# Four interleaved attention layers on one core: the linear layers' second pass in halves of the array's rows

## The chip, the cores and the metric

The kernel runs on one core of one Trainium2 chip. The metric is the device time of one execution in microseconds (us), the median of several runs. PE is the matrix engine, PEld its weight loads, DVE the vector engine, ACT the scalar engine, POOL the GpSimd engine and SP the engine that issues most DMAs.

## The reference

Four layers follow each other, A, B, A, B, each with a residual sum, on x of 2048 tokens and 512 features, 32 heads of 16. The A layers are linear attention; the change is in them. (B is softmax attention in four segments with a compressive memory; it is not touched.)

```
def _A_ref(x, wqkv, w_phi, wo):          # x is layer-normed
    q, k, v = split((x @ wqkv))          # each [heads 32, tokens 2048, 16]
    pq = einsum("hsd,hdf->hsf", q, w_phi);  pk = the same of k
    phi_q = concat([softmax(pq), softmax(-pq)])      # 32 features a head
    phi_k = concat([softmax(pk), softmax(-pk)])
    kv = einsum("hsf,hsd->hfd", phi_k, v);  z = sum over s of phi_k
    num = einsum("hqf,hfd->hqd", phi_q, kv)
    den = einsum("hqf,hf->hq", phi_q, z) + 1e-6
    return (num / den) @ wo
x = x + _A_ref(_layernorm(x), ...)
```

All numbers are fp32; large products are split into a high and a low fp32r part and done as three products.

## The kernel before, in words

A layer A works in tiles of 128 tokens, 16 of them (NT). Its first pass makes keys, values and the raw queries' features, and sums over all tokens, for each head, 32 features by 17 columns (16 of kv and one of z). These sums become KN, a tile of 128 rows (4 heads of 32 features) by 8 groups by 4 x 17 columns, where each head's rows are zero outside its own 17 columns.

The second pass, `pass2`, is what the change touches. For each tile i it does these steps, in this order in the text of the program:

1. `turn`: the divided outputs o of tile i-1 are transposed on PE (four 128x128 blocks into one PSUM bank), ACT copies the high part, DVE subtracts the low part (tiles oh, ol).
2. `exp` on ACT of the features of tile i+2.
3. For i of 12 and more, `transposed(i+1)` stands here; see step 5.
4. KN: two halves of 4 groups. Each group is two products, of 128 feature rows by 64 tokens each, against all 68 columns of KN's group, at column positions 0 and 64 of the array. After each half, `weigh` divides by the 17th column on DVE (reciprocal r, then a product into o).
5. For i = 0 and i = 3 to 11, `transposed(i+1)`: the features of tile i+1 (1024 columns) are transposed on PE in eight 128x128 blocks into the two banks of the PSUM tile lg, and ACT copies them out (tile P).
6. `differences` on POOL for tile i+3, then `scale_q` of tile i+2: sums es on DVE (behind its exp), the ratio rr on DVE, and a product on POOL that scales one half of the features. Only after it can `transposed` of that tile run.
7. Loads of the raw features of tile i+4 and of the residual rows.
8. `out_proj` of tile i-1: 12 products of 128x128 by 512 on PE, then a sum with the residual rows x on DVE straight from PSUM, and the store. For i = 1 and 2, `transposed(i+1)` stands behind it.

The second pass is a generator; after most of the steps it yields. The main loop takes its first 110 steps (A20), and between them, at the step numbers in STEPS, one step of the next B layer's opening (weights, layer norm, four transposes a tile). One tile is nine steps. The remaining steps are dealt out into early slots of layer B.

The order of the instructions on each engine is fixed: `held` ties every PE instruction to the one traced before it, and the wrapper `Ordered` does so for DVE, ACT, POOL and SP. So each engine works in the order in which the program text calls it. PSUM has the tags g (4 banks), lg (one tile of two banks), mx and my (one bank each). All matrix products are recorded at the line of `mm` (L177), transposes at that of `tp` (L181), and everything on the four wrapped engines at L155.

Of the kernel before, what the change touches and what calls it, by code (L numbers as in the profile page):

```python
# [7 lines left out]
F32 = mybir.dt.float32  # L8
F32R = mybir.dt.float32r
# [9 lines left out]
P = 128  # L19
NSEG = 4  # L20
NC = D // P
NT = T // P
VW = DH + 1
# [6 lines left out]
OO = 4  # L30
UU = 3
MT = 1
G = 4
# [68 lines left out]
def interleave_kernel(ctx, tc, x_in, a_wqkv, a_wphi, a_wo, b_wq, b_wk, b_wv, b_wo, b_beta,  # L102
                      c_ident, c_mask, c_bd, out):
    nc = tc.nc
    MUL, ADD, SUB, MAX, MIN = ALU.mult, ALU.add, ALU.subtract, ALU.max, ALU.min
# [10 lines left out]
    def nm(s):  # L116
        uid[0] += 1
        return f"{s}_{uid[0]}"

    def T2(tag, bufs, dt=F32, shape=(P, 512)):  # L120
        return sp.tile(list(shape), dt, tag=tag, bufs=bufs, name=nm(tag))

    def PS(tag, bufs, shape=(P, 512)):
        return ps.tile(list(shape), F32, tag=tag, bufs=bufs, name=nm(tag))
# [7 lines left out]
    def wait(f):  # L132

        if put_off[0] is None:
            f()
        else:
            put_off[0].append(f)

    def behind(i, j):

        tc.add_manual_dep(i.ins, j.ins.name,
                          mybir.DependencyInfo(mybir.DependencyClass.NoSync, mybir.DependencyReason.DATA),
                          reason="keeps order")
# [19 lines left out]
    dve, act, pool, sync = [Ordered(e) for e in (nc.vector, nc.scalar, nc.gpsimd, nc.sync)]  # L163

    def held(i):

        if last[0] is not None:
            behind(i, last[0])
        last[0] = i
        return i  # L170

    work = [0.0]

    def mm(*a, **k):
        n = a[0].free_size()
        work[0] += n / 2.26 if k["rhs"].dtype == F32R else (n * 2 / 2.4 + 25 if "tile_position" in k else 2 * max(112, n * 2 / 2.4))
        return held(nc.tensor.matmul(*a, **k))  # L177

    def tp(*a):
        work[0] += 108  # L180
        return held(nc.tensor.transpose(*a))  # L181

    def dma(out, in_):
        sync.dma_start(out=out.bitcast(F32), in_=in_.bitcast(F32))

    ident = cp.tile([P, P], F32, name="ident")
# [248 lines left out]
    def mm3(po, lhs, rhs, kcs=range(NC)):  # L435

        for kc in kcs:
            for n, (a, b) in enumerate(((0, 0), (0, 1), (1, 0))):
                mm(po, lhsT=lhs(a, kc), rhs=rhs(b, kc), start=(kc == kcs[0] and n == 0),
                   stop=(kc == kcs[-1] and n == 2))  # L440
            if kc < kcs[-1]:
                yield
# [32 lines left out]
    def turn(ot):  # L475

        o = [T2("oh", OO, F32R), T2("ol", OO, F32R)]
        pt = PS("g", G)
        for c, block in enumerate(ot):
            tp(pt[:, c * P : (c + 1) * P], block, ident)  # L480
        pt, hi, lo = [t[:, 0 : len(ot) * P] for t in (pt, *o)]
        act.copy(hi, pt)
        wait(lambda: dve.tensor_tensor(out=lo, in0=pt, in1=hi.bitcast(F32), op=SUB))
        return o

    turns = [0]

    def residual(xsrc, i, spare, every=4):
# [5 lines left out]
    def out_proj(x, xdst, i, o, w):  # L494
        po = PS("g", G)
        yield from mm3(po, lambda a, kc: o[a][:, kc * P : (kc + 1) * P], lambda b, kc: w[b][:, kc, :])

        def end():
            dve.tensor_tensor(out=x, in0=po, in1=x, op=ADD)
            sync.dma_start(out=xdst[i], in_=x)  # L500
        wait(end)
        yield

    def out_pair(tiles, xdst, w, soon, late, w0=0, w1=D):
# [15 lines left out]
    def weigh(out, p, eps, add, eng=pool):  # L520

        n, G = out.shape[1], out.shape[2]
        r = T2("r", 4, shape=(P, n, G))
        den = p[:, :, :, DH]
        if eps:
            dve.tensor_scalar(r, den, eps, None, op0=ADD)
            den = r
        dve.reciprocal(r, den)
        rb = r.unsqueeze(3).broadcast_to([P, n, G, DH])
        if not add:  # L530
            dve.tensor_tensor(out=out, in0=p[:, :, :, 0:DH], in1=rb, op=MUL)
            return
        t = T2("wt", 1, shape=(P, n, G, DH))
        dve.tensor_tensor(out=t, in0=p[:, :, :, 0:DH], in1=rb, op=MUL)
        eng.tensor_tensor(out=out, in0=out, in1=t, op=ADD)
# [71 lines left out]
    def differences(p, mm):  # L607

        pv = p.rearrange("p (h f) -> p h f", f=DH)
        e = T2("P4", NP4, shape=(P, H, 2, DH))  # L610
        pool.tensor_tensor(out=e[:, :, 0, :], in0=pv,
                                in1=mm[:, 0, :].unsqueeze(2).broadcast_to([P, H, DH]), op=SUB)
        pool.tensor_tensor(out=e[:, :, 1, :],
                                in0=mm[:, 1, :].unsqueeze(2).broadcast_to([P, H, DH]), in1=pv, op=SUB)
        return e

    def exp(e):
        ef = e.rearrange("p h s f -> p (h s f)")
        act.activation(ef, ef, AF.Exp)
# [24 lines left out]
    class LayerA:  # L644
# [267 lines left out]
        def pass2(self):  # L912

            KN = self.KN
            phT = {}

            def transposed(i):

                if i >= NT:
                    return
                ef = self.e.pop(i).rearrange("p h s f -> p (h s f)")
                phT[i] = T2("P4", NP4, shape=(P, 8, P))
                pt = PS("lg", 1, (P, 2, 512))
                for half in range(2):
                    for q in range(4):
                        g = 4 * half + q
                        tp(pt[:, half, q * P : (q + 1) * P], ef[:, g * P : (g + 1) * P], ident)
                    if half == 1:  # L930
                        act.copy(phT[i].rearrange("p g t -> p (g t)"), pt.rearrange("p h x -> p (h x)"))
                    yield

            yield from transposed(0)
            o = None
            self.rest = []
            for i in range(NT):
                if 0 < i <= NT - 4:
                    oT = turn([o[:, c * P : (c + 1) * P] for c in range(NC)])
                    yield  # L940
                soon = [i + 2] if i < NT - 5 else [i + 2, i + 3] if i == NT - 5 else [i + 3]
                soon = [n for n in soon if n < NT]
                for n in soon:
                    exp(self.e[n])
                o = T2("ot", OT) if NT - 4 <= i else T2("U", UU)
                if i >= NT - 4:
                    yield from transposed(i + 1)
                f = phT.pop(i)
                for half in range(2):
                    pn = PS("g", G)  # L950
                    pv = pn[:, 0 : 16 * VW].rearrange("p (g h e) -> p g h e", g=4, h=4)
                    for q in range(4):
                        g = 4 * half + q
                        for a in (0, 64):
                            mm(pn[a : a + 64, q * 4 * VW : (q + 1) * 4 * VW], lhsT=f[:, g, a : a + 64],
                               rhs=KN[:, g].rearrange("p h e -> p (h e)"), start=True, stop=True,
                               tile_position=(0, a))
                    weigh(o[:, half * 256 : half * 256 + 256].rearrange("p (g h d) -> p g h d", g=4, h=4),
                          pv, 0.0, False)
                    yield  # L960
                if i == 0 or 2 < i < NT - 4:
                    yield from transposed(i + 1)
                if i == 0:
                    self.begun(3)
                for n in [i + 3] if i < NT - 6 else [i + 3, i + 4] if i == NT - 6 else [i + 4]:
                    if n < NT:
                        self.e[n] = differences(*self.raw.pop(n))
                for n in soon if i != 1 else ():
                    scale_q(self.e[n])
                for n in [i + 4] if i < NT - 7 else [i + 4, i + 5] if i == NT - 7 else [i + 5]:  # L970
                    self.load_q(n)
                if i < NT - 4:
                    ahead = residual(self.xsrc, i, ("ot", OT))
                else:
                    self.rest.append(o)
                if 0 < i <= NT - 4:
                    yield from out_proj(x, self.xdst, i - 1, oT, self.wo)
                if 0 < i < 3:
                    yield from transposed(i + 1)
                if i == 1:  # L980
                    scale_q(self.e[i + 2])
                x = ahead
# [621 lines left out]
```

## Time and profile before

| | us |
|---|---|
| median of 3 runs | 1316.24 |
| lowest, highest | 1312.12, 1317.13 |
| the profiled execution, its time | 1313.56 |
| its span, first to last instruction | 1311.8 |
| busy in it: PE | 1269.2 |
| DVE | 1075.4 |
| ACT | 835.4 |
| POOL | 758.6 |

The page's groups name an instruction by its tiles, written <- read. `g<-KN,P` are the products with KN, `lg<-ident,P` the transposes of features, `g<-ident,U` those of outputs, `g<-w,oh` and `g<-w,ol` the output projection, `es` and `rr` the sums and ratios on DVE, `P<-P,rr` the scaling on POOL. A fp32 product is recorded as two. In the timeline a row gives start, length, engine, line, operation, tiles and a count of merged instructions; in square brackets stand the engine's idle time before it and what ended that.

### The profile page before, as it was taken

The page shows a single profiled execution, that of the slowest core. Times are in us where ns is not written, and L with a number is a line of the kernel's source. Part 1 is how long each engine was busy: PE and PEld are TensorE (multiplying, and loading weights), DVE is VectorE, ACT ScalarE, POOL GpSimd, SP SyncE. Part 2 cuts the span into 40 slices and gives each one's busy share as a digit, 9 for nine tenths or more (in the row PEclk, how much of TensorE's full clock was granted, in tenths as well). Part 3 has the DMA queues.
Part 4 walks back from the last instruction along what each step waited for, and adds up shares of the span by engine and source line. Part 5 has one row for each costly group of instructions (what it writes and reads, how often), then busy time and mean ns, then how long its engine had stood idle before and what let it go on. Part 6 is the DMA issues. An engine that isn't in the chain of part 4 may idle for free.

```text
span 1311.8 us, 41989 instructions
## 1 busy us (share of the span) xinstructions
PE 1269.2 (97%) x16488; PEld 991.8 (76%) x16488; DVE 1075.4 (82%) x3499; ACT 835.4 (64%) x1210; POOL 758.6 (58%) x1124
## 2 busy tenths in 40 slices
PE   7999989999999999999999999899999999999987
PEld 6887878877777777777668887787877777777765
DVE  4776778788998998998857767787899899898895
ACT  5556435648788788776644433465678878877754
POOL 2568755425757768666324446563356766766653
PEclk9999999999999999999999999999999999999999
DMA  6387538545655545545441103565546545544432
GB/s 212 105 318 257 171 126 245 168 121 156 186 160 153 160 126 141 159 134 156 131 161 65 65 33 130 169 202 153 154 127 208 173 130 153 143 137 114 122 84 81
DMA packets 134420, 196.59 MB, mean 150 GB/s; under 512 B 15440, under 2 KB 61648, under 8 KB 133456
## 3 DMA queue, kind: packets, MB, share of 16 engines
q1 hardware_dynamic: 133408, 193.80, 48.9%
q8 instruction: 131, 2.15, 0.7%
q14 instruction: 65, 0.53, 0.1%
q10 hardware_dynamic: 816, 0.11, 0.1%
HBM read 101.05 MB, written 39.85 MB: 107 GB/s over the span
## 4 chain that ended last, share of the span: by engine, by line
PE 79%; DVE 14%; ACT 2%; issue 2%; DMA 2%; POOL 1%; SPq 0%; DVEq 0%; ACTq 0%; POOLq 0%
PE g L177 62%; PE lg L177 6%; PE g L181 4%; PE mx L177 3%; DVE g L155 2%; DVE U L155 2%; PE lg L181 2%; DVE mx L155 2%; DVE my L155 1%; ACT P L155 1%; PE my L177 1%; DVE es L155 1%; POOL P L155 1%; DVE mxs L155 1%; DMA P<-in 1%
## 5 line engine op out<-in xcount | busy, mean ns | idle before, releaser
L155 ACT ACTIVATE P<-lg 128x1024 f32<-128x1024 f32 x316 | 324.3, 1026 | 97.7 <-PE lg L177 75.9
L155 POOL TENSOR_SCALAR_AFFINE_SELECT P<-P 128x256 f32<-128x256 f32 (+1 forms) x448 | 190.8, 444 | 228.7 <-ACT P L155 209.3
L155 DVE CUSTOM_DVE_ANT_0 g<-g,mask 128x128 f32<-128x128 f32 (+3 forms) x392 | 189.4, 537 | 7.2 <-PE g L177 6.7
L155 DVE CUSTOM_DVE_ANT_0 mx<-mx,mask 128x512 f32<-128x512 f32 (+2 forms) x316 | 158.6, 502 | 38.1 <-PE my L177 26.3
L177 PE MATMUL g<-hh,wqk 64*128 64x512 f32 (+1 forms) x960 | 185.0, 392 | 0.7 <-SPq L155 0.3
L177 PE MATMUL g<-w,oh 64*128 64x512 f32 (+2 forms) x848 | 163.5, 382 | 3.1 <-ACT oh L155 2.6
L155 DVE CUSTOM_DVE_ANT_0 my<-my,mask 128x512 f32<-128x512 f32 (+2 forms) x316 | 163.3, 517 | 0.0
L177 PE MATMUL lg<-e,e 64*128 64x512 f32 (+1 forms) x1010 | 147.1, 344 | 7.6 <-ACT P L155 7.5
L177 PE MATMUL g<-P,v 128*32 128x128 f32 (+3 forms) x2064 | 151.7, 433 | 0.2
L177 PE MATMUL g<-w,hh 64*128 64x512 f32 (+1 forms) x672 | 143.2, 395 | 2.5 <-ACT w L155 1.3
L155 DVE DVE_READ_ACCUMULATOR2_ANT mxs<- 128x1 f32 x1024 | 142.4, 139 | 0.0
L177 PEld LDWEIGHTS lg<-e,e 64*128 64x128 f32 x1010 | 93.4, 184 | 51.7 <-ACT P L155 20.1
L177 PEld LDWEIGHTS g<-hh,wqk 64*128 64x128 f32 (+1 forms) x960 | 102.7, 185 | 18.1 <-SPq L155 1.6
L177 PEld LDWEIGHTS g<-P,v 128*32 128x32 f32 x2064 | 65.5, 109 | 60.9 <-issue 53.3
L177 PEld LDWEIGHTS g<-w,oh 64*128 64x128 f32 (+1 forms) x848 | 96.2, 188 | 19.8 <-ACT oh L155 3.5
L177 PE MATMUL g<-hl,wqk 64*128 64x512 f32 (+1 forms) x480 | 103.8, 389 | 0.0
L177 PE MATMUL g<-w,ol 64*128 64x512 f32 (+2 forms) x424 | 102.7, 379 | 0.5 <-DVE ol L155 0.5
L155 ACT COPY tb<-g 128x512 f32<-128x512 f32 (+1 forms) x132 | 71.2, 576 | 43.9 <-PE g L177 42.1
L177 PEld LDWEIGHTS g<-w,hh 64*128 64x128 f32 (+1 forms) x672 | 82.9, 187 | 19.2 <-ACT w L155 1.6
L177 PE MATMUL g<-w,hl 64*128 64x512 f32 (+1 forms) x336 | 88.7, 392 | 0.0
L155 DVE TENSOR_REDUCE es<-P 128x64 f32<-128x1024 f32 x64 | 77.3, 1209 | 13.1 <-ACT P L155 13.1
L155 POOL TENSOR_TENSOR ta<-tb,ta 128x512 fp32r<-128x512 f32 x60 | 76.3, 1292 | 14.0 <-ACT ta L155 11.2
(163 smaller groups left out, 2944.6 us busy)
## 6 DMA issues: line engine op xcount, KB each, us to landing
e<-ta SPq DMA_DIRECT2D x384, 128.0 KB
wqk<-wqk SPq DMA_DIRECT2D x128, 256.0 KB
x<-x SPq DMA_DIRECT2D x48, 256.0 KB
pq<-tb SPq DMA_DIRECT2D x24, 256.0 KB
tb<-pq SPq DMA_DIRECT2D x24, 256.0 KB
x<-xr SPq DMA_DIRECT2D x22, 256.0 KB
xr<-x SPq DMA_DIRECT2D x20, 256.0 KB
x<-in SPq DMA_DIRECT2D x16, 256.0 KB
```

The costliest lines, as they stand in the source:

```text
L155: i = f(*a, **k)
L177: return held(nc.tensor.matmul(*a, **k))
L181: return held(nc.tensor.transpose(*a))
```

## The change

- `tp_halves` is new: a block of 128 rows is transposed as two halves of 64 rows, at row positions 0 and 64 of the array, into two different PSUM banks.
- `transposed` and the new `turn_halves` use it: 16 half transposes for the features, 8 for the outputs. The outputs' halves go to the banks mx and my instead of g, and are copied by two ACT copies and two DVE subtractions of 128x256. The B layer keeps using `turn`.
- KN: each group is two products again, but now each takes 64 feature rows (two heads) by all 128 tokens, against the 34 columns of these two heads, at row positions 0 and 64; the two go to two banks of g. The division of both stands behind the second half.
- `transposed(i+1)` stands ahead of KN for i of 3 and more (it was behind it for 3 to 11).
- `out_proj`: ACT copies the product to a tile y (tag U), POOL adds the residual rows, then the store.

```
+    def tp_halves(outs, in_):
+        work[0] += 74
+        for row, out in zip((0, 64), outs):
+            held(nc.tensor.transpose(out, in_[row : row + 64], ident[row : row + 64, row : row + 64],
+                                     tile_position=(row, 0)))
...
+    def turn_halves(o):
+        hi, lo = T2("oh", OO, F32R), T2("ol", OO, F32R)
+        pts = [PS(t, 1)[:, 0 : NC * 64] for t in ("mx", "my")]
+        for c in range(NC):
+            tp_halves([pt[:, c * 64 : (c + 1) * 64] for pt in pts], o[:, c * P : (c + 1) * P])
+        views = [[t.rearrange("p (c r x) -> p r c x", c=NC, r=2)[:, r] for t in (hi, lo)]
+                 + [pts[r].rearrange("p (c x) -> p c x", c=NC)] for r in range(2)]
+        for h, _, pt in views:
+            act.copy(h, pt)
+        def low():
+            for h, l, pt in views:
+                dve.tensor_tensor(out=l, in0=pt, in1=h.bitcast(F32), op=SUB)
+        wait(low)
+        return hi, lo
...
     def out_proj(x, xdst, i, o, w):
...
-        def end():
-            dve.tensor_tensor(out=x, in0=po, in1=x, op=ADD)
-            sync.dma_start(out=xdst[i], in_=x)
-        wait(end)
+        y = T2("U", UU)
+        act.copy(y, po)
+        pool.tensor_tensor(out=x, in0=y, in1=x, op=ADD)
+        sync.dma_start(out=xdst[i], in_=x)
         yield
...
                 for half in range(2):
-                    for q in range(4):
-                        g = 4 * half + q
-                        tp(pt[:, half, q * P : (q + 1) * P], ef[:, g * P : (g + 1) * P], ident)
+                    for g in range(4 * half, 4 * half + 4):
+                        tp_halves([pt[:, r, g * 64 : (g + 1) * 64] for r in range(2)], ef[:, g * P : (g + 1) * P])
                     if half == 1:
-                        act.copy(phT[i].rearrange("p g t -> p (g t)"), pt.rearrange("p h x -> p (h x)"))
+                        act.copy(phT[i].rearrange("p g (r t) -> p r g t", r=2),
+                                 pt.rearrange("p r (g t) -> p r g t", g=8))
...
-                    oT = turn([o[:, c * P : (c + 1) * P] for c in range(NC)])
+                    oT = turn_halves(o)
...
-                if i >= NT - 4:
+                if 2 < i:
                     yield from transposed(i + 1)
                 f = phT.pop(i)
+                pns = [PS("g", G)[:, 0 : 16 * VW] for _ in range(2)]
                 for half in range(2):
-                    pn = PS("g", G)
-                    pv = pn[:, 0 : 16 * VW].rearrange("p (g h e) -> p g h e", g=4, h=4)
-                    for q in range(4):
-                        g = 4 * half + q
-                        for a in (0, 64):
-                            mm(pn[a : a + 64, q * 4 * VW : (q + 1) * 4 * VW], lhsT=f[:, g, a : a + 64],
-                               rhs=KN[:, g].rearrange("p h e -> p (h e)"), start=True, stop=True,
-                               tile_position=(0, a))
-                    weigh(o[:, half * 256 : half * 256 + 256].rearrange("p (g h d) -> p g h d", g=4, h=4),
-                          pv, 0.0, False)
+                    for g in range(4 * half, 4 * half + 4):
+                        for r, pn in enumerate(pns):
+                            row = slice(64 * r, 64 * r + 64)
+                            mm(pn[:, g * 2 * VW : (g + 1) * 2 * VW], lhsT=f[row, g, :],
+                               rhs=KN[row, g, 2 * r : 2 * r + 2, :].rearrange("p h e -> p (h e)"),
+                               start=True, stop=True, tile_position=(64 * r, 0))
+                    if half == 1:
+                        for r, pn in enumerate(pns):
+                            weigh(o.rearrange("p (g r h d) -> p r g h d", g=8, r=2, h=2)[:, r],
+                                  pn.rearrange("p (g h e) -> p g h e", g=8, h=2), 0.0, False)
                     yield
-                if i == 0 or 2 < i < NT - 4:
+                if i == 0:
                     yield from transposed(i + 1)
```

## The prediction, made before the changed kernel was run

> **What bounds the kernel now.** I read the page's shares first, then the windows of the second pass tile by tile, then one tile in the timeline.
>
> ```profile
> span 1311.8 us, 41989 instructions
> PE 1269.2 (97%) x16488; PEld 991.8 (76%) x16488; DVE 1075.4 (82%) x3499; ACT 835.4 (64%) x1210; POOL 758.6 (58%) x1124
> ```
>
> ```profile
> core 0: us, PE busy (x) PEld busy (x) DVE busy (x) ACT busy (x) POOL busy (x), PEclk, DMA share, GB/s
> 204.24:209.60 5.36, 5.36 (x60) 4.53 (x57) 4.23 (x10) 2.56 (x4) 1.98 (x2) 1.00 0.87 241
> ...
> 198.88:248.73 49.85, 49.45 (x492) 41.34 (x489) 42.86 (x94) 27.81 (x37) 29.49 (x36) 1.00 0.64 199
> 178.94:250.85 71.91, 67.75 (x717) 56.99 (x717) 60.05 (x129) 37.60 (x49) 43.20 (x50) 0.98 0.55 169
> 820.88:890.46 69.58, 66.53 (x717) 55.66 (x717) 58.09 (x125) 37.94 (x49) 42.87 (x50) 1.00 0.55 175
> ```
>
> PE is busy 97% of the span. The second pass of the two linear layers runs alone (with the next layer's opening) from 178.94 to 250.85 and from 820.88 to 890.46. From the feature turns of tile 4 at 198.88 to those of tile 13 at 248.73 there are nine tiles in 49.85 us, with PE idle for 0.4; a plain tile takes 5.36 us. Counting PE alone would be natural, but one tile shows a second chain close behind.
>
> ```profile
> 207.69 1.06 POOL L155 TENSOR_TENSOR P<-P,rr 128x512 f32<-128x512 f32 x1 [2.53 <-DVE rr L155]
> 207.97 0.60 PE L181 MATMUL g<-ident,U 128*128 128x128 f32 x4
> 208.50 1.17 PE L177 MATMUL g<-KN,P 128*64 128x68 f32 x32
> 209.60 1.09 PE L181 MATMUL lg<-ident,P 128*128 128x128 f32 x8
> 210.44 0.71 PE L177 MATMUL g<-w,oh 128*128 128x512 f32 x2
> 209.83 0.25 DVE L155 RECIPROCAL r<-g 128x16 f32<-128x16 f32 x1
> 211.08 1.21 DVE L155 TENSOR_REDUCE es<-P 128x64 f32<-128x1024 f32 x1
> 212.71 0.19 DVE L155 TENSOR_TENSOR rr<-rr,es 128x32 f32<-128x32 f32 x1
> 213.04 1.06 POOL L155 TENSOR_TENSOR P<-P,rr 128x512 f32<-128x512 f32 x1 [1.27 <-DVE rr L155]
> 213.33 0.60 PE L181 MATMUL g<-ident,U 128*128 128x128 f32 x4
> 214.96 1.09 PE L181 MATMUL lg<-ident,P 128*128 128x128 f32 x8
> ...
> 226.09 0.86 PEld L181 LDWEIGHTS lg<-ident,P 128*128 128x128 f32 x8 [0.48 <-POOL P L155]
> ```
>
> This is i = 5: outputs of tile 4 turned (207.97), tile 5 times KN (208.50), features of tile 6 turned (209.60), output projection until 213.33. On DVE, tile 5's outputs are divided from 209.83, and only behind that come tile 7's sums (es, 211.08), its ratio rr, and Pool's scaling, 213.04 to 214.10. Tile 7's features are turned at 214.96, 0.86 after. At 226.09 the turn already waits 0.48 for Pool. From the end of KN's products (208.50 + 1.17 = 209.67) to the end of the scaling: 4.43 us. Before the change this is no loop of one tile: the turn stands behind KN, so a late turn(i+1) does not delay KN(i), the head of the next scaling.
>
> **The change part by part.**
>
> *The turn of tile i+1 moves ahead of KN(i), for i = 3 to 11 (it stood there already from i = 12).* Now turn(i+1) needs the scaling issued in iteration i-1; KN(i) stands behind turn(i+1) on PE, as does the output projection; the division of tile i waits for KN(i); on DVE es(i+2) stands behind the division; and turn(i+2) waits for its scaling. The loop closes once a tile: turn, KN, then the 4.43 us above. The generators' steps per tile stay nine, so the next layer's opening falls at the same steps; none falls between KN's second half and es.
>
> *KN by half rows.* Prices:
>
> ```profile
> L177 PEld LDWEIGHTS lg<-e,e 64*128 64x128 f32 x1010 | 93.4, 184 | 51.7 <-ACT P L155 20.1 <-issue 13.0 <-ACT ta L155 4.1
> L177 PEld LDWEIGHTS g<-e,w 128*128 128x128 f32 x192 | 35.7, 188 | 8.2
> L177 PEld LDWEIGHTS g<-KN,P 128*64 128x64 f32 x1024 | 33.4, 138 | 12.5 <-ACT P L155 8.6 <-issue 2.7 <-DVE ot L155 0.3
> L177 PEld LDWEIGHTS g<-mem,tb 128*32 128x32 f32 x3072 | 31.5, 109 | 12.5 <-DVE mxs L155 9.2 <-issue 3.3
> L181 PEld LDWEIGHTS lg<-ident,P 128*128 128x128 f32 x256 | 28.1, 141 | 7.2 <-POOL P L155 4.4 <-issue 0.9
> L177 PE MATMUL g<-mem,tb 128*32 128x34 f32 x3072 | 36.9, 199 | 2.8 <-DVE mxs L155 2.8
> L177 PE MATMUL lg<-phibd,e 128*128 128x128 f32 x32 | 4.1, 280 | 0.0
> ```
>
> Before, 16 products per tile (two passes each, 32 records) load 64 columns and stream 68. After, again 16 products and 32 records, but each loads 128 columns of 64 rows and streams 34. Loads go by columns: 109 ns for 32, 138 for 64, 188 for 128; and half the rows save next to nothing (184). So the stream shrinks and the load grows by 184 - 138 = 46 to 50 ns. KN now takes 208.50 to 209.60, 1.10 us for 16 pairs, 69 ns a pair. If the pair is paced by its load, 16 x 48 = 0.77 is added: 1.94 us to the last product's end in place of 1.17. Lower end: the loads hide wholly and only 34-column streams count, 36.9 / 3072 = 12 ns, 32 of them 0.38 plus some 0.2 of drain, 0.58. Upper end: phibd's full 128-column products, 4.1 / 32 = 128 ns a pair, 2.05. I take 1.94, as the 64x128 load is the row nearest to it.
>
> The Trainium skill ("TensorE: Matmul & The Clock Gate", section "LDWEIGHTS (loading the stationary operand)") says the same against this change: a load takes its columns over 1.2 ns, whatever the rows. By it a pair grows by 53 ns where I took 48 and KN to 2.02, the total about 1343; the rows 184 and 188 agree.
>
> *Turns by halves.* A turning load of 128 columns (141) lasts no longer than KN's of 64 (138), and the stream halves to 64 columns; so I take KN's pair of today, 69 ns, against 0.84 for eight (209.60 to the next product at 210.44): features 8 x 0.069 = 0.55, outputs 0.28 for about 0.43. Bounds: no gain, 0.84; or 34-column pace, 0.2. PE gains 0.45 a tile here and loses 0.77 in KN.
>
> *Copies and residual sums.*
>
> ```profile
> L155 DVE TENSOR_TENSOR ol<-g,oh 128x512 fp32r<-128x512 f32 x32 | 21.8, 687 | 7.6 <-ACT oh L155 7.5
> L155 DVE TENSOR_TENSOR U<-g,r 128x256 f32<-128x256 f32 x48 | 20.4, 424 | 1.6
> L155 DVE TENSOR_TENSOR xr<-g,xr 128x512 f32<-128x512 f32 x12 | 8.3, 689 | 7.7 <-PE g L177 7.7
> L155 ACT COPY U<-g 128x512 f32<-128x512 f32 x32 | 19.0, 593 | 35.7 <-PE g L177 32.5 <-issue 3.2
> L155 POOL TENSOR_TENSOR xr<-tb,xr 128x512 f32<-128x512 f32 (+1 forms) x18 | 22.7, 1262 | 0.0
> ```
>
> The low parts in two halves cost DVE 2 x 0.424 for 0.687, 0.16 more, spent while DVE waits for KN: nothing. The halved ACT copies add at most one start (bounded by 0.59), under KN too: nothing, since the exponentials then end before the division does. The 24 residual sums leave DVE (0.69 each), at a place where DVE waits anyway: no gain. ACT gets 24 copies of 0.59 and Pool 24 sums of 1.26. On Pool the sum stands behind the scaling of the same iteration and ahead of the next two differences (each as wide as the scaling's 1.06): 1.26 + 2.12 after a scaling is over well within a loop of 6.9, before the next ratio comes. SP's store waits for Pool's sum instead of DVE's; the loads queued behind it feed later tiles. All hidden by the longer loop; without that cover the Pool sum would be the 1.26. The products' output in two banks per tile, divided only after both halves, starts the first division at KN's end; the 4.43 is counted from there.
>
> *The sum.* Loop = 0.55 + 1.94 + 4.43 = 6.92 us, against 49.85 / 9 = 5.54 now; PE's own work, 5.36 - 0.45 + 0.77 = 5.68, fits inside, so PE idles about 1.2 a plain tile. The first loop's start hangs on KN(2):
>
> ```profile
> 178.94 1.17 PE L177 MATMUL g<-KN,P 128*64 128x68 f32 x32 [1.50 <-DVE KN L155]
> 182.14 1.57 PE L181 MATMUL lg<-ident,P 128*128 128x128 f32 x8 [2.03 <-POOL P L155]
> 184.85 1.71 PE L177 MATMUL g<-KN,P 128*64 128x68 f32 x32 [0.29 <-ACT P L155]
> 191.59 1.17 PE L177 MATMUL g<-KN,P 128*64 128x68 f32 x32 [0.72 <-ACT P L155]
> ...
> 282.41 2.34 PE L177 MATMUL g<-KN,P 128*64 128x68 f32 x64
> ...
> 815.66 0.21 PE L177 MATMUL my<-v,P 128*32 128x17 f32 x2 [3.10 <-issue]
> ```
>
> ```profile
> core 0: us, PE busy (x), PEclk, DMA share, GB/s
> 815.80:819.20 3.40, 3.40 (x19) 1.00 0.74 268
> 182.20:184.00 1.80, 1.80 (x11) 0.61 0.00 0
> ```
>
> ```profile
> 363.06 0.40 PE L177 MATMUL g<-hh,wqk 64*128 64x512 f32 x2
> ```
>
> KN(2) at 191.59 + 0.77 (KN(1)) - 0.45 (turns) = 191.9; its end 193.85; turn(4) at 198.3. Nine loops: 260.6. Turn(13) and KN(12), 0.55 + 1.87 (1.94 less the tail): 263.0, where 250.85 stood: +12.1 a layer. The three KN blocks left over (two of them at 282.41) and two feature turns run among the next layer's PE work: 3 x 0.77 - 2 x 0.3 = +1.7. Two layers: 27.6. On the profiled execution's 1313.56 (span 1311.8 and 1.8 around it): 1341. That execution is 2.7 under the median of 1316.24; on the median the sum gives 1344, and I forecast 1342.
>
> **The rivals.**
> - *Loads hide (other side).* KN 0.58: loop 5.56, turn(4) at about 195.6 (after tile 3's copy out of the one lg buffer), KN(12) done at 246.7, -4.2 a layer, the rest -2.7: 1300. For it: two 64-row products of 512 columns take 0.40 together (363.06), hardly more than one. Against: 184 ns for half rows. It decides where KN falls under some 0.9.
>  The Trainium skill ("TensorEngine Tiling (Array Packing)", section "Theoretical Speedup") gives up to 2x where a dimension is 64 or less; halving 1.17 gives 0.58, this rival's price and its 1300. No run here shows it for 34 columns.
> - *KN costs as now, 1.17.* Loop 6.15, turn(4) at 196.8, end 253.8: +2.9, rest -0.6: 1318, the same.
> - *The loop isn't closed* (sums get ahead of the division on DVE): PE bound, 5.68 a tile, about +3.2 and +1.7 a layer: 1323. Against: es stands right behind the division in every tile.
> - *The clock drops in the new gaps.* After idles of 1.50 and 2.03 the granted clock was 0.61, the feature turns took 1.57 for 1.09 and KN 1.71 for 1.17: some 1 to 1.5 us an event; after 3.10 idle at 815.66 it stayed at 1.00. A third of the 18 loops: +9, 1350; all: 1368.
>
> **How the numbers follow.** Load-paced loop 0.68 (1333 to 1350 by turns of 0.84 or 0.2 and KN of 1.7 to 2.05); clock 0.10; loop open 0.04; KN as now 0.10; loads hide 0.08. Under 0.5% can't be told from no change: the three runs spread 0.4%. Slower 0.68 + 0.10 + 0.04 + a third of KN as now = 0.85; same 0.08; faster 0.07. The range 1318 to 1360 leaves out the hidden loads, half of KN as now, and a deep clock drop.
>
> **What would show it.** Turn(i+1) waits for Pool about 1.2 us in each of tiles 4 to 13, in both layers; tiles of about 6.9; KN 1.9 and its loads near 184 ns; feature turns 0.55; DVE and Pool idle longer. Wrong if PE stays full in 198 to 249, or if the KN block takes 1.2 or less.

## The result, and the profile after

The changed kernel takes 1355.51 us (median of 4 runs, 1351.9 to 1365.49) where the kernel before took 1314.18 beside it: a ratio of 1.0326, 95% interval 1.0301 to 1.0352, so 3.3% slower. The profiled execution is the fastest of the four, 1351.9 us with a span of 1350.2.

The page of the changed kernel, its head and shares, and its row of the granted clock (40 equal slices, tenths of full speed):

```profile
span 1350.2 us, 42757 instructions
PE 1292.6 (96%) x16840; PEld 1014.6 (75%) x16840; DVE 1063.7 (79%) x3499; ACT 848.6 (63%) x1258; POOL 786.8 (58%) x1148
PEclk9999989999999999999999999999899999999999
```

PE is busy 23 us more than before, but the span grew by 38. The windows of the second pass of the first linear layer say where: one plain tile, five of them, four stretches to which I come back under the clock, and the whole pass up to its last product.

```profile
core 0: us, PE busy (x) PEld busy (x) DVE busy (x) ACT busy (x) POOL busy (x), PEclk, DMA share, GB/s
207.29:214.20 6.91, 5.87 (x68) 4.88 (x69) 3.72 (x10) 3.13 (x6) 4.33 (x5) 1.00 0.67 189
207.29:241.85 34.56, 29.36 (x340) 24.36 (x340) 21.51 (x53) 15.84 (x27) 22.99 (x29) 1.00 0.65 194
180.28:183.69 3.41, 2.50 (x56) 2.37 (x54) 1.65 (x5) 1.60 (x2) 0.45 (x1) 1.00 0.00 0
183.69:190.52 6.83, 6.83 (x46) 6.09 (x42) 6.09 (x14) 1.70 (x3) 5.17 (x5) 0.50 0.01 4
296.33:299.75 3.42, 3.42 (x64) 3.26 (x63) 3.35 (x15) 1.01 (x1) 0.00 (x0) 1.00 0.88 204
299.75:306.57 6.82, 6.82 (x38) 5.73 (x37) 4.71 (x22) 1.02 (x1) 0.41 (x1) 0.50 0.07 15
...
178.00:266.54 88.54, 76.78 (x885) 64.85 (x884) 54.49 (x129) 46.09 (x74) 55.68 (x59) 0.94 0.45 138
```

A plain tile takes 6.91 us where it took 5.36, and no engine is full in it: PE works 5.87 of the 6.91, DVE 3.72, POOL 4.33. That is what a closed chain looks like in a profile. The timeline of that stretch (start, length, engine; in brackets the idle time before and who ended it) shows its links:

```profile
213.09 1.06 POOL L155 TENSOR_TENSOR P<-P,rr 128x512 f32<-128x512 f32 x1 [2.58 <-DVE rr L155]
214.20 0.71 PE L187 MATMUL lg<-ident,P 64*128 64x64 f32 x16 [1.03 <-POOL P L155]
214.75 1.93 PE L177 MATMUL g<-KN,P 64*128 64x34 f32 x32
216.71 0.26 DVE L155 RECIPROCAL r<-g 128x16 f32<-128x16 f32 x1 [2.25 <-PE g L177]
218.04 1.21 DVE L155 TENSOR_REDUCE es<-P 128x64 f32<-128x1024 f32 x1
220.01 1.05 POOL L155 TENSOR_TENSOR P<-P,rr 128x512 f32<-128x512 f32 x1 [2.59 <-DVE rr L155]
221.11 0.20 PEld L187 LDWEIGHTS lg<-ident,P 64*128 64x128 f32 x4 [1.18 <-POOL P L155]
```

Each engine waits for the one above it: the turn 1.03 us for Pool's scaling, the division 2.25 for PE's products, the next scaling 2.59 for the ratio, the next turn 1.18 (its loads) for Pool. From one turn to the next it is 221.11 - 214.20 = 6.91. The second layer's tiles take 6.92.

The groups of instructions for what was re-shaped, two of the kernel before and three of the changed one (count | total busy us, mean ns of one | idle before them):

```profile
L177 PE MATMUL g<-KN,P 128*64 128x68 f32 x1024 | 37.9, 228 | 6.5 <-ACT P L155 5.0 <-DVE KN L155 1.5
L181 PE MATMUL lg<-ident,P 128*128 128x128 f32 x256 | 35.5, 281 | 2.8 <-POOL P L155 2.7
...
L177 PE MATMUL g<-KN,P 64*128 64x34 f32 x1024 | 68.2, 286 | 4.1 <-ACT P L155 4.1
L177 PEld LDWEIGHTS g<-KN,P 64*128 64x128 f32 x1024 | 66.0, 203 | 4.9 <-ACT P L155 4.7
L187 PE MATMUL lg<-ident,P 64*128 64x64 f32 x512 | 23.2, 228 | 17.4 <-POOL P L155 15.4 <-ACT P L155 2.0
```

The products with the keys' sums went from 37.9 us of PE time to 68.2 although each streams half as many columns (their loads, 33.4, to 66.0); the feature turns came down from 35.5 to 23.2 and now wait 15.4 us for Pool, where the wait was 2.7.

### The profile page after: what moved, and what is told of

Read it like the earlier page. It is cut to its first block, busy times and chain, and to the rows that moved or that the text cites. A ratio compares the mean times of both kernels' runs of the same rounds, so it can differ in the third digit from the quotient of the medians.

```text
span 1350.2 us, 42757 instructions
## 1 busy us (share of the span) xinstructions
PE 1292.6 (96%) x16840; PEld 1014.6 (75%) x16840; DVE 1063.7 (79%) x3499; ACT 848.6 (63%) x1258; POOL 786.8 (58%) x1148
## 4 chain that ended last, share of the span: by engine, by line
PE 79%; DVE 13%; issue 2%; POOL 2%; ACT 2%; DMA 2%; SPq 0%; DVEq 0%; POOLq 0%; ACTq 0%
PE g L177 63%; PE lg L177 6%; PE mx L177 3%; PE g L181 3%; DVE U L155 3%; DVE g L155 2%; DVE es L155 2%; PE my L177 1%; POOL P L155 1%; PE lg L187 1%; DVE mx L155 1%; DVE my L155 1%; ACT P L155 1%; DVE r L155 1%; DMA P<-in 1%
## 5 line engine op out<-in xcount | busy, mean ns | idle before, releaser
L177 PE MATMUL g<-w,oh 64*128 64x512 f32 (+2 forms) x848 | 166.3, 385 | 2.6 <-ACT oh L155 2.6
L177 PEld LDWEIGHTS g<-hh,wqk 64*128 64x128 f32 (+1 forms) x960 | 99.9, 186 | 19.5 <-SPq L155 2.2
L155 ACT COPY U<-g 128x512 f32<-128x512 f32 x56 | 33.0, 590 | 102.5 <-PE g L177 99.4
```

The source lines that it names most:

```text
L155: i = f(*a, **k)
```

## The experiments

Theory: the turn ahead of the products closes a loop of one tile, and the load-paced half-row products lengthen it. First rival: the order is harmless and the slow products carry all the loss.

### One part undone, one part done alone

The order alone put back (`e1`), the order alone taken over into the kernel before (`e2`), and the half-row products alone (`e3`):

```
e1, against the changed kernel:
-                if 2 < i:
+                if i >= NT - 4:
                     yield from transposed(i + 1)
...
-                if i == 0:
+                if i == 0 or 2 < i < NT - 4:
                     yield from transposed(i + 1)

e2, against the kernel before: the same two lines the other way round

e3, against the kernel before: the loop of KN products and its `weigh`
as in the change; turns, order and residual sums as before
```

> The changed kernel with one thing undone: in tiles 3 to 11 the features of tile i+1 are turned behind the product with the keys' sums again, not ahead of it. Half turns, half-row products and Pool's residual sums stay. Loop theory: the chain turn, product, division, sums of the queries, scaling, next turn is open again; the tile then costs what the array itself does, 29.36/5 = 5.87 us in place of 6.91, nine tiles in each of two layers: 1355.5 - 18.7 = about 1337 us (1328 to 1343), and the feature turns no longer show about 1 us of waiting for Pool. Rival, that the loss lies in the slower products alone (and in the clock they bring): the order is worth nothing, 1350 to 1358 us.

> The kernel before with one thing done: in tiles 3 to 11 the features of tile i+1 are turned ahead of the product with the keys' sums. Whole turns, products by columns and VectorE's residual sums stay. Loop theory: turn 0.85 + product 1.10 to 1.17 + 4.43 from the product's end to the scaling's end = 6.4 to 6.45 us a tile for 5.54, nine tiles, two layers: 1314 + 15 to 16 = about 1330 us (1324 to 1336), with turns that wait some 0.9 us a tile for Pool. Rival, that the order is harmless as long as the products are short: 1311 to 1318 us.

> The kernel before with one thing done: the products with the keys' sums go by halves of the array's rows. Whole turns, the old order and VectorE's residual sums stay. Theory that the loads set the pace: the product takes 1.93 us for 1.10, and since the array had 0.04 us idle in a tile of 5.54, all of the 0.83 us shows: nine tiles, two layers, and part of the other seven tiles, 1314 + 15 to 24 = 1329 to 1338 us. Rival, that half-row products hide their loads when no loop holds them up: 1305 to 1316 us. On the clock: if the load-paced products lower it, stretches of 3.4 or 6.8 us at half clock stand near them in this run too, as in the changed kernel (seven), and not three as before.

Measured, against the kernel before on the same chip (1313.8): e1 1334.63, ratio 1.0165 (1.0141 to 1.0189); e2 1323.61, 1.0076 (1.0058 to 1.0094); e3 1341.83, 1.0214 (1.0187 to 1.0241). The timelines give the tile, from feature turn to feature turn; e1, e2 and e3:

```profile
210.82 0.69 PE L187 MATMUL lg<-ident,P 64*128 64x64 f32 x16
216.50 0.69 PE L187 MATMUL lg<-ident,P 64*128 64x64 f32 x16
```

```profile
208.78 1.09 PE L181 MATMUL lg<-ident,P 128*128 128x128 f32 x8 [0.49 <-POOL P L155]
209.81 1.17 PE L177 MATMUL g<-KN,P 128*64 128x68 f32 x32
210.55 0.26 DVE L155 RECIPROCAL r<-g 128x16 f32<-128x16 f32 x1 [0.91 <-PE g L177]
214.89 1.09 PE L181 MATMUL lg<-ident,P 128*128 128x128 f32 x8 [0.48 <-POOL P L155]
```

```profile
207.08 1.09 PE L181 MATMUL lg<-ident,P 128*128 128x128 f32 x8
213.25 1.09 PE L181 MATMUL lg<-ident,P 128*128 128x128 f32 x8
```

- e1: with the old order the wait for Pool is gone, the tile takes 5.68 us and PE has no gap. 20.9 us of the loss go with two moved `if`s. The rival falls.
- e2: the order alone costs 9.8 us in a kernel whose products are fast. The tile is 6.11 with a wait of 0.49 for Pool at each turn: the loop, without any half-row product. I had expected 6.4; the old products fill one bank per half, so the first division starts at 210.55, 0.43 before the last product's end at 210.98, while the changed kernel divides after both halves (216.71, behind the products' end at 216.68). That is a small cost of the change that I had put into the 4.43 without seeing that the old form did not have it. The time is just under the 1324 to 1336 that I had given.
- e3: PE stays full and each tile takes 6.17 for 5.36, which is the 0.81 by which the products grew (1.17 to 1.98). The products are as slow without the loop as in it. The time went 4 us over the upper end that I had given; the mean clock of its profile is 0.992, to which I come back under the clock.

### The loop opened in another way

`e4` leaves PE's order as in the change and reorders DVE: in tiles 2 to 11 the sums and the ratio of tile i+2 stand ahead of the division of tile i.

```
+                rrs = {n: ratio_q(self.e[n]) for n in soon} if 1 < i < NT - 4 else {}
                 for half in range(2):          # KN products, weigh
...
-                    scale_q(self.e[n])
+                    scale_q(self.e[n], rrs.get(n))
```

> The changed kernel with VectorE's order changed in tiles 2 to 11: the sums and reciprocals for the queries of tile i+2 stand ahead of the division of tile i, and no longer behind it. TensorE, Pool and the turns keep their order and shapes. Loop theory: the scaling then does not wait for the product any more, the loop is open and the tile costs the array's 5.87 us: about 1337 us (1328 to 1345). Rival, that the turn ahead of the product waits for Pool for another reason (Pool's own queue, with the residual sum in it): turns still wait about 1 us and the time stays at 1350 to 1358 us.

Measured 1350.71 (1342.61 to 1358.27), ratio 1.0280 (1.0233 to 1.0326). In the timeline and the windows of e4:

```profile
203.87 0.71 PE L187 MATMUL lg<-ident,P 64*128 64x64 f32 x16 [1.00 <-ACT P L155]
209.58 0.66 PE L187 MATMUL lg<-ident,P 64*128 64x64 f32 x16
215.24 0.66 PE L187 MATMUL lg<-ident,P 64*128 64x64 f32 x16
221.13 0.71 PE L187 MATMUL lg<-ident,P 64*128 64x64 f32 x16
...
241.03 0.69 PE L187 MATMUL lg<-ident,P 64*128 64x64 f32 x16
```

```profile
203.87:221.13 17.26, 17.19 (x205) 14.45 (x206) 11.25 (x27) 8.68 (x15) 11.97 (x14) 1.00 0.72 220
241.03:250.25 9.22, 9.22 (x80) 7.82 (x76) 3.70 (x9) 5.25 (x9) 3.86 (x4) 0.63 0.33 116
```

The loop is open: 5.71, 5.66 and 5.89 us a tile, PE busy 17.19 of 17.26, no wait for Pool. So the wait did come by way of DVE's order, and the rival that named Pool's own queue falls for these tiles. But the time did not follow. Later tiles are longer (6.38, 7.50, and one of 9.22 with the clock at 0.63), and in the waits of 205 to 240 us Pool now waits 3.7 us for loads of saved queries. My 1337 was wrong by 14: a chain that is opened lets the next lateness show, and the mean clock, 0.976, is the lowest of all the profiles. The execution in the profile, 1358.27 us, is the slowest of e4's four, so its late tiles show more than the median has.

### The clock

The granted clock is 0.50 in stretches of 3.41 us or a multiple of it. The mean clock over the span gives their price if PE sets the pace throughout: (1 - 0.986) x 1350.2 = 18.9 us in the changed kernel, (1 - 0.996) x 1311.8 = 5.2 in the one before.

```profile
core 0: 1350.2 us, clock 0.986
```

Two places recur in the other kernels. One is the start of the pass (183.69 to 190.52), behind a stretch with PE busy 2.50 of 3.41 us. The other is the end: the last two tiles' products stand back to back, and the profile shows PE busy all through 296.33 to 299.75 (3.42 of 3.42), and yet the clock is 0.50 from 299.75 to 306.57. No idle time that the profile shows can be the reason there. (It counts a product as busy from start to end, 286 ns on the mean, while one starts every 60 ns; so the row doesn't tell an array that streams from one that waits for loads.) Single stretches of 3.41 us stand at 252.0, late in the loop, and at 924.4, behind the second layer's, after windows with PE busy 2.85 and 2.99 of 3.41. All five kernels with 34-column products (the changed one, e1, e3, e4, e10) have a stretch that begins within their last products or right behind them, in both layers (299.7 and 958.5 us; 292.4 and 944.3; 294.4 and 946.3; 300.4 and 962.6; 298.1 and 963.7). None of the kernels with column products has one there. `e6` keeps loads, order and count of products and lets each stream 64 columns (the division reads the same 34 of them):

```
-                            mm(pn[:, g * 2 * VW : (g + 1) * 2 * VW], lhsT=f[row, g, :],
-                               rhs=KN[row, g, 2 * r : 2 * r + 2, :].rearrange("p h e -> p (h e)"),
+                            mm(pn[:, g * 64 : (g + 1) * 64], lhsT=f[row, g, :],
+                               rhs=KN[row, g].rearrange("p h e -> p (h e)")[:, 4 * r : 4 * r + 64],
```

> The changed kernel with the same half-row loads, order and count of products, but each product streams 64 columns in place of 34 (the additional columns are not used). Theory that the loads set the products' pace: a block stays at 1.93 us (up to 2.0) and the loop at 6.91 us a tile. Rival on the pace: the streams matter, the block grows to 2.4 us or more, the loop to 7.4. On the clock, theory that it is given by how much the array streams, not by whether it is occupied: the low stretches after the last products of each layer (299.7 and 958.5 us in the changed kernel) go, and the time falls to 1340 to 1350 us. Rival, that half-row products lower the clock whatever they stream: the stretches stay, 1350 to 1358 us.

Measured 1344.22, ratio 1.0234 (1.0209 to 1.0260): 11 us faster than the changed kernel by streaming almost twice the columns. The windows around the same place in e6, and two turns of its loop:

```profile
295.22:300.00 4.78, 4.78 (x87) 4.66 (x84) 4.59 (x18) 1.01 (x1) 0.00 (x0) 1.00 0.67 156
300.00:307.00 7.00, 7.00 (x52) 5.49 (x49) 5.56 (x24) 3.57 (x4) 0.95 (x3) 1.00 0.04 8
```

```profile
213.81 0.71 PE L187 MATMUL lg<-ident,P 64*128 64x64 f32 x16 [1.05 <-POOL P L155]
220.76 0.71 PE L187 MATMUL lg<-ident,P 64*128 64x64 f32 x16 [1.05 <-POOL P L155]
...
295.72 3.93 PE L177 MATMUL g<-KN,P 64*128 64x64 f32 x62
```

The tile is 6.95 us, as with 34 columns (6.91), and a block 1.95 for 1.93: the stream doesn't set the pace. That the loads do is the reading that is left, by their 66.0 us of the products' 68.2; no run has half-row products with loads of fewer columns. The stretches at 299.7 and 958.5 are gone, and the four runs of e6 have mean clocks of 0.992 to 0.994 where the changed kernel's have 0.975 to 0.986. The added columns are zeros of KN, so it was not their values that kept the clock up. What the clock follows is then not whether PE counts as busy but something that grows with the columns streamed. The mean clock of e6's profile is 0.992, worth 10.7 us by the same product; of the 18.9, 8.2 are gone, where the profiled span fell by 7.3. The stretch at the start of the pass stays, and two of 3.4 us are new, at 884.0 and 897.6, behind windows in which PE was busy for 2.35 and 2.36 of 3.40 us; why is open.

The other traces bear the reading out, though not as a sharp rule. I count the columns of PE's records in windows of 3.41 us, laid end to end from the drops, between 20 and 1295 us. In the fourteen traces 50 windows at full clock have a drop behind them; in 49 of these PE streamed at most 4176 columns, as in 164 of the 4853 others, and in 8 it shows no idle time. The window from 296.33 had 3288 columns with PE busy throughout and lost the clock; windows of the loop with 3968 and PE busy for 2.38 of 3.41 (211.00 to 214.41) kept it; e6's two windows over its last products had 5376 each. One of e1 with 4176 lost it and one of e6 with 3328 kept it, so what exactly counts stays open.

### The rest of the change, and a better kernel

`e8` is the kernel before with the residual sums on Pool; `e11` has the half turns alone; `e5` has both, with column products and the old order; `e7` is e5 with the turn ahead and the sums first; `e10` is the changed kernel with the residual sums back on DVE. Their edits are whole parts of the change's diff, done or undone; the sums first are e4's edit.

> The kernel before with one thing done: the residual sums of the output projection go through a copy on ScalarE to Pool. Turns, products and order are those of before. Theory that they are hidden either way, since the array paces the tile: 1311 to 1317 us, ratio within 0.3%. Rival 1, that Pool's longer queue (1.27 us more in a tile) delays the scalings: over 1318 us. Rival 2, that VectorE's relief shortens the tile: under 1309 us.

> The changed kernel with two of its parts undone: the products with the keys' sums go by columns again, and in tiles 3 to 11 the features of tile i+1 are turned behind them. What stays of the change: half turns of features and outputs, and the residual sums on Pool. By the parts measured so far (rows alone +19.7 us, rows with half turns and Pool +8.2, both with the low-clock time taken off the spans) these two are worth some -11.5 us: 1314 - 11 = about 1303 us (1298 to 1308); a tile of 5.36 us should take 4.9 to 5.1, since the array saves 0.29 on a feature turn and 0.15 on an output turn. Rival, that another engine's chain ends the tile as soon as the array is shorter: 5.3 us a tile and 1310 to 1315. On the clock: no low stretch after the last products of either layer (some 115 us behind the start of the second pass), where the four kernels with half-row products had one and the two with column products none.

> Of the change, the half turns of features and outputs alone: products by columns, the old order, VectorE's residual sums. Theory that the array paces the tile, and that the 2.5 us and 0.5 us of waiting for Pool in tiles 7 and 9 of the run with Pool's sums came from loads of the queries that stood behind a store waiting for Pool: 5.14 us in every tile from 4 to 11 for 5.36 (5.77 and 5.90 in two), some 0.22 in 14 tiles of two layers: 1314 - 6 = about 1308 us (1304 to 1311). Rival, that the tile ends elsewhere once the array is shorter, whoever adds the residual: 1312 to 1317 us.

> The changed kernel with one part undone and one order changed: products by columns again, and on VectorE the sums and reciprocals of the queries of tile i+2 ahead of the division of tile i (tiles 2 to 11). The features are still turned ahead of the product. By the loop theory the chain is open, as the 5.66 us a tile of the run with the sums first showed for 6.91, and with a block of 1.10 for 1.93 a tile takes 4.9 to 5.1 us: about 1302 us (1296 to 1308). Rival, that with the turn ahead the chain of scaling, turn and exponentials is the next bound, at 5.4 us or more a tile: 1310 to 1316 us.

> The changed kernel with one part undone: VectorE adds the residual again, straight from the accumulator, with no copy on ScalarE and nothing on Pool. Theory that this part is covered while the loop of turn, product, division and scaling paces the tile: 6.9 us a tile (6.85 to 6.95) and 1352 to 1358 us. Rival 1, that it costs here what it costs alone (1317.7 for 1314.0): 1348 to 1352 us. Rival 2, that VectorE's sum of 0.6 to 0.7 us comes between the division and the queries' sums, in the loop: 7.3 to 7.6 us a tile and over 1362 us.

| kernel | median us | ratio to before, 95% |
|---|---|---|
| e8: Pool's sums | 1317.70 | 1.0021 (1.0006 to 1.0037) |
| e5: Pool's sums, half turns | 1317.17 | 1.0021 (1.0006 to 1.0037) |
| e1: and half-row products | 1334.63 | 1.0165 (1.0141 to 1.0189) |
| the change: and the turn ahead | 1355.51 | 1.0326 (1.0301 to 1.0352) |
| e11: half turns | 1313.31 | 0.9988 (0.9974 to 1.0002) |
| e7: half turns, Pool's sums, turn ahead, sums first | 1321.81 | 1.0052 (1.0032 to 1.0072) |
| e10: the change, sums on DVE | 1356.55 | 1.0326 (1.0298 to 1.0354) |

The first four rows are a ladder, one part at a time: +0.2, 0.0, +1.4, +1.6%. e10 confirms that under the long loop Pool's sums cost nothing (its tile is 6.84 us). Alone they do cost something: e8 came just above the 1311 to 1317 that I had given. I had expected e5 at 1303 and e11 at 1308; both missed. Its tiles do shrink, to 5.14 (203.93, 209.07, 214.22); then one waits. Timelines of e5: PE, Pool, and SyncE's queue.

```profile
214.22 0.71 PE L187 MATMUL lg<-ident,P 64*128 64x64 f32 x16
221.94 0.71 PE L187 MATMUL lg<-ident,P 64*128 64x64 f32 x16 [2.52 <-POOL P L155]
...
214.24 1.29 POOL L155 TENSOR_TENSOR xr<-U,xr 128x512 f32<-128x512 f32 x1
218.80 1.06 POOL L155 TENSOR_TENSOR P<-tb,mmq 128x512 f32<-128x512 f32 x1 [3.27 <-DMA tb<-pq]
...
215.56 0.50 SPq L155 DMA_DIRECT2D x<-xr  x1
...
217.34 0.89 SPq L155 DMA_DIRECT2D tb<-pq  x1
```

The store (x<-xr) waits for Pool's sum, which ends at 215.53; the load of saved queries (tb<-pq) stands behind it and is issued at 217.34; Pool waits 3.27 us for it, and PE 2.52 for Pool. In e11, with DVE's sum, the store goes out at 213.10, the load at 214.85, and the same turn still waits 1.11 us. Two kernels try to remove that: `e14` is e5 with the store issued from Pool's queue, `e15` is e11 with each load one tile earlier in SyncE's queue.

```
e14:  -        sync.dma_start(out=xdst[i], in_=x)
      +        pool.dma_start(out=xdst[i], in_=x)
e15:  -                for n in [i + 4] if i < NT - 7 else [i + 4, i + 5] if i == NT - 7 else [i + 5]:
      +                for n in [4, 5] if i == 0 else [i + 5] if i < NT - 7 else [NT - 2, NT - 1] if i == NT - 7 else []:
```

> The kernel with half turns, column products, the old order and Pool's residual sums (1317.2 us), with one thing more: the store of the sum is issued from Pool's queue, right behind the sum, and no longer from SyncE's, where the next load of queries stands behind it. Queue theory: the loads of the queries are on time, the 2.5 us of waiting for Pool in tile 7 goes, in both layers, and with it some of tile 9's: 1317 - 6 = about 1311 us (1306 to 1313). Rival 1, that Pool itself is late, with 1.28 us more in a tile: 1315 to 1320 us. Rival 2, that the issue takes Pool's time, some 1 us a tile: over 1320 us.

> The kernel with half turns alone (products by columns, old order, VectorE's residual sums; 0.9988 of the kernel before), with one thing more: in the second pass each load of saved query rows is put into SyncE's queue one tile earlier, ahead of one more store. Theory that what is left of the half turns' gain was lost to late loads (Pool waited 3.83 us for one at 216.8 us, TensorE 1.1 us for Pool at 219.9): that wait goes in both layers, every tile from 4 to 8 takes 5.14 us, and the ratio falls to 0.995 to 0.997, about 1310 us beside 1315 of before. Rival, that the queue is full of the next stage's transfers there and the order of two entries does not matter: the wait stays over 0.8 us and the ratio at 0.998 to 1.001.

e14: 1320.35, ratio 1.0040 (1.0026 to 1.0054). e15: 1315.17, ratio 0.9992 (0.9979 to 1.0006). Timelines of e14 and e15:

```profile
219.66 0.71 PE L187 MATMUL lg<-ident,P 64*128 64x64 f32 x16 [0.40 <-POOL P L155]
226.13 0.71 PE L187 MATMUL lg<-ident,P 64*128 64x64 f32 x16 [1.26 <-POOL P L155]
232.99 0.71 PE L187 MATMUL lg<-ident,P 64*128 64x64 f32 x16 [1.66 <-POOL P L155]
...
210.05 0.58 POOL L155 DMA_DIRECT2D x<-xr  x1 [0.30 <-POOL xr L155]
```

```profile
213.88 0.71 PE L187 MATMUL lg<-ident,P 64*128 64x64 f32 x16
219.08 0.71 PE L187 MATMUL lg<-ident,P 64*128 64x64 f32 x16
224.94 0.71 PE L187 MATMUL lg<-ident,P 64*128 64x64 f32 x16 [0.65 <-POOL P L155]
```

In e14 the wait of 2.52 falls to 0.40, and 1.26 and 1.66 appear in the next tiles: each issue takes Pool 0.58 us and 0.30 of waiting. In e15 the 1.11 falls to nothing (the tile is 5.20) and 0.65 appears in the next one. In both the wait that the edit aimed at shrank and others appeared; neither gained time. e7 missed too: its tiles run from 5.03 to 8.02, and Pool, whose residual sum now stands ahead of work that is ready, waits 4.1 us for ScalarE's copies; ahead of the longest tile it waits another 3.56, for which no run names the cause. The half turns save 0.22 us in a plain tile, but e11's interval touches 1.000. No version here is surely faster than the kernel before.

## Why the prediction was right

1342 was forecast, in a range of 1318 to 1360, with slower at 0.85; 1355.5 came. The mechanism was the forecast one; one size in it was right by luck, and the clock was missing. By its steps:

- **The loop.** Forecast 0.55 + 1.94 + 4.43 = 6.92 us a tile; measured 6.91, with the wait for Pool at every turn of the stretch (forecast about 1.2, measured 1.03). From KN's end to the scaling's end, 216.68 to 221.06, it is 4.38. PE's own work was put at 5.68; e1 runs at 5.68. e1 and e4 open the loop in two ways and the wait goes in both.
- **The products.** Forecast load-paced at 1.94 us; measured 1.93. The direction came from the load rows of before: 184 ns for half the rows with 128 columns against 138 for 64 columns. The size is luck in part. The sum charged the 48 ns once for each of the 16 products, but the rows list two loads a product (1024 in 32 blocks, 32 a block); 32 x 48 ns would have given 2.7 us. Loads overlap: each lasts 189 ns, and one starts every 60 (1.93 / 32), where it was every 34 (1.10 / 32). So a load added 26 ns and not 48. The upper end of 2.05 took phibd's 32 records for 32 pairs; by its row 16 pairs take 4.1 us. (The rival of hidden loads has a rest of -2.7 that is -2.4 by its own terms; its 1300 stands.) The Trainium skill ("TensorE: Matmul & The Clock Gate", section "LDWEIGHTS (loading the stationary operand)") lets a load's time go by columns and not by rows; the trace agrees on the rows (a median of 189 ns for the products' 64 by 128, a mean of 188 for 128 by 128 before; in the turns 140 for 64 by 128, 141 for 128 by 128 before). But 128 columns take 189 ns in the products and 140 in the turns, so the columns alone don't give the time. e6 shows that between 34 and 64 columns the stream doesn't matter. The rival that loads hide is refuted by e3's 6.17.
- **The turns.** 0.55 forecast, 0.55 measured (214.20 to 214.75).
- **Pool's sums.** Nothing, as forecast, under the cover of the loop (e10); without it some 3 us in all (e8), and not 1.26 a tile. One way is SyncE's queue, where the store holds up a load (e5; e8 has such a wait of 0.83 us at 220.01). I had looked at that queue and passed it over. It isn't all: behind the pass of e8, PE waits 1.85 and 1.78 us (264.25 and 905.96) for ACT, which the kernel before doesn't do there. Which part is which no run separates.
- **The clock, the term that was mis-sized.** The sum was 27.6 us and carried nothing for it; the profiled span grew by 38.4. By the mean clock, 18.9 - 5.2 = 13.7 of this is granted-clock loss at most, which leaves 24.7. The forecast had it as a rival at 0.10, with a third of the loops at half clock for 1350. Its 9 us were near, its mechanism was not: in the loop's gaps of 1.03 us the clock stayed at 1.00 (207.29 to 241.85). It fell where the short products follow each other, at the end of the pass with no gap that the profile shows. The Trainium skill (same page, section "What's actually happening") ties the slow state to an idle window of some 3.4 us; the stretches here have that length, but the window ahead of the one at 299.75 shows no idle time. Here the measurement decides: a PE that counts as busy throughout with short streams did not hold the clock, and with streams of 64 columns it did.
- **The end of the pass.** KN(12) was forecast done at 263.0, and was at 266.54. In that pass the mean clock is 0.94, worth (1 - 0.94) x 88.54 = 5.3 us at most, where before it was 0.98 of 71.91, 1.4: the 3.9 between cover the 3.5 that were missed. 2.1 of these had come before the loop: turn(4) was forecast at 198.3 and stood at 200.41, behind the half-clock stretch from 183.69. The last two tiles' products, 2.34 us before and put at 3.88, took over 5:

```profile
297.05 5.09 PE L177 MATMUL g<-KN,P 64*128 64x34 f32 x63
```

At full clock, in e6, 62 of them take 3.93.

So the forecast was right by its main mechanism, and short by 13.5 us. On the profiled execution the sum gave 1341 and 1351.9 came; the clock's 13.7 at most cover these 10.7. The median lies 3.6 above that execution, and the other runs have lower mean clocks than its 0.986 (0.984, 0.982, 0.975). The clock had been treated as a matter of gaps.

## What to carry to other kernels

Here, splitting a product into row halves traded columns streamed for columns loaded. Before such a split, compare the load rows by their columns, take the spacing of the loads and not their length, and ask what the short streams do to the granted clock. Before work is moved ahead on an in-order engine, follow its result round through the other engines' orders: if it comes back to the same point within one iteration, the sum of that circle, and not the busiest engine, is the time of the iteration. A store that waits in an in-order DMA queue delays the load behind it, so a sum moved to a slower engine can be paid for where that load is used.

## What the runs showed of the hardware that I had not expected

- The clock fell to 0.50 behind 3.42 us in which the profile shows no idle time of PE, and didn't where the same loads came with 64 columns of stream for 34; the wider streams cost next to nothing in the loop (6.95 for 6.91 us a tile) and made the whole 11 us faster.
- Two loads of the same form, 64 rows by 128 columns, went at different rates: sixteen of the turns in 0.55 us, 34 ns each, and thirty-two of the products in 1.93 us, 60 ns each. Twice as many loads of half the rows paid for the turns (0.84 to 0.55); the same count of loads with half the rows and twice the columns did not pay for the products (1.10 to 1.93). Why the turns' loads are quicker is open.
